# Quarter-array attention, nine-token loads and one set of buffers in an attention and expert-routing kernel

## The chip, the cores and the metric

The kernel runs on 1 core of one Trainium2 chip. The metric is device time in microseconds (us), lower is better. A core has TensorE (PE, matrix products), VectorE (DVE), ScalarE (ACT), GpSimd (POOL), a queue engine (SP), and 16 DMA engines that move data between its memory (SBUF) and DRAM. PE writes its results into PSUM, eight banks of 2 KB a partition; SBUF and PSUM have 128 partitions.

## The reference

```python
# q, k, v: (8 batches, 8 heads, 576 tokens, 64), float32; g_norm: (64,)
kv  = np.einsum('bhsd,bhse->bhde', k, v)
out = np.einsum('bhsd,bhde->bhse', q, kv)
rms = np.sqrt(np.mean(out * out, axis=-1, keepdims=True) + 1e-06)
x   = (out / rms * g_norm)            # transposed and reshaped to (4608 tokens, 512)

logits = x @ w_gate                   # 8 experts
expert_idx = np.argmax(logits, axis=1)
gate_w = softmax(logits)[expert_idx]  # one number a token
for e in range(8):                    # w1: (8, 512, 1024), w2: (8, 1024, 512), float32
    mask = expert_idx == e
    h = np.maximum(x[mask] @ w1[e], 0.0)
    out[mask] = gate_w[mask, None] * (h @ w2[e])
```

Linear attention without a softmax, a norm per head, and then each token goes to one of eight experts. With the given inputs the experts get 564, 494, 600, 572, 539, 654, 585 and 600 tokens.

## The kernel before, in words

The order of the work on every engine is written by hand (`manual_schedule`): each engine does its instructions in the order of the program text, and semaphores hold an instruction until its inputs are there.

**Attention** works in 36 steps `s` of 128 tokens, nine for each pair `P` of batches. `load_qkv` (L157) brings 512 tokens of a batch, four tokens a partition, as rows of 1 KB; `load_rem` (L165) brings the other 64 tokens of two batches as rows of 256 B. All are issued by SP. `heads` (L192) lets POOL copy q into an order by heads. `kv_mm` (L200) multiplies k and v on PE into `kvp`; `kv_copy` (L221), `kv_t` (L227) and `kv_gate` (L235) make from it the blocks `kvs`: for two heads a block diagonal of 128 x 128 and, beside it, 16 columns that give the gate's logits.

A step does: `x_mm` (L267, PE: q transposed times `kvs`, in four products of 128x144), `x_qt` (L251, PE: transposes q for step s + 2), `x_norm` (L284: ACT squares, DVE sums, then in `rest` ACT's Ln and Exp give the inverse root, and DVE writes logits `lr` and tokens `xg` in f16), `x_qs` (L263, ACT: copies the transposed q to SBUF). The lists `mid`, `late` and `last` put the k-v work of later batches, the loads, the casts and the routing into given steps.

`Route` (L318) finds, for nine steps at once (4, 3 and 2 at the end), the best expert of each token (`first`, DVE), its rank among the tokens of that expert (`ranks`, PE), and sends the tokens to rows of `xs_scratch` in DRAM by one indirect DMA of POOL a step (`send`, L386). Unused rows are blanked at the start (L443). After the last step `left_over_table` (L494) finds the tokens over 640 of an expert.

**Experts.** A `Job` (L553) is one expert with room for 5 x 128 = 640 tokens. `fetch` (L562, SP) reads its rows with a transposing DMA; `one` (L581) does four matmuls of 128x320 and ACT's relu; `two` (L600) does eight matmuls of 128x512 for 128 tokens, DVE scales the result, and POOL writes it to its tokens' rows by an indirect DMA (L611). Tokens over the room are done by one more job of 128, ahead of the last expert, and by a loop at the end for further ones. `Weights` (L119): `stage` loads w1 in f32 by SP into one buffer `wst`, `scale` casts it with `g_norm` to f16 (POOL for the first two experts, then DVE), `second` loads w2 by POOL's queue with a cast to f16 on the way. The experts have buffers of their own, which take the place of the attention's when that is closed.

Of the kernel before, what the change touches and what calls it, by code (L numbers as in the profile page):

```python
# [28 lines left out]
def kernel(  # L29
# [20 lines left out]
    CAP = CT * 128  # L50
    NOV = (N - CAP) // 128
# [19 lines left out]
    o = 144 + CT  # L71
    for P in range(4):
        for bb in range(2):
            for j in range(4):
                c32[:, o + 9 * P + 4 * bb + j] = (2 * P + bb) * S + 4 * ar + j
        c32[:64, o + 9 * P + 8] = 2 * P * S + 512 + ar[:64]
        c32[64:, o + 9 * P + 8] = (2 * P + 1) * S + 512 + ar[:64]
# [13 lines left out]
    P_w = ctx.enter_context(tc.tile_pool(name="pw", bufs=1))  # L91

    cf = P_const.tile([128, c32.shape[1]], F32, tag="cf")
    ch = P_const.tile([128, 384], F16, tag="ch")
# [10 lines left out]
    wg = P_const.tile([128, 4, 8], F32, tag="wg")  # L105
    g2 = P_const.tile([128, 1], F32, tag="g2")
    gw = P_const.tile([128, 4, 2, 8], F32, tag="gw")
    epsb = P_const.tile([128, 1], F32, tag="epsb")
    csum = P_const.tile([128, 8], F32, tag="csum")
    valid = P_const.tile([128, E, CT], F32, tag="valid")  # L110
    bigm = P_const.tile([128, E, CT], F32, tag="bigm")
    nvf = P_const.tile([128, 32], F32, tag="nvf")
    tabb = P_const.tile([128, 32], F32, tag="tabb")
    xo_bufs = [P_const.tile([128, RW], F16, tag=f"xo{n}", name=f"xo{n}") for n in range(2)]
    tabi = P_const.tile([128, 2, 32], I32, tag="tabi")
    blank = P_const.tile([96, RW], I32, tag="blank")


    class Weights:  # L119
        def __init__(self, e):  # L120
            self.e = e if isinstance(e, bass.DynSlice) else slice(e, e + 1)

        def stage(self):
            self.st = P_w.tile([128, 4, F], F32, tag="wst", bufs=1, name="wst")
            nc.sync.dma_start(
                self.st, moe_w1[self.e, :, :].rearrange("o (t p) f -> p (o t) f", p=128)
            )

        def scale(self, eng, kk):
            if kk == 0:  # L130
                self.w1 = P_w.tile([128, 4, F], F16, tag="w1e", bufs=3, name="w1e")
            eng.tensor_scalar(  # L132
                self.w1[:, kk, :], self.st[:, kk, :], g2, 1.0, op0=ALU.mult, op1=ALU.mult
            )

        def second(self):
            self.w2 = P_w.tile([128, 8, D], F16, tag="w2e", bufs=3, name="w2e")
            nc.gpsimd.dma_start(
                self.w2, moe_w2[self.e, :, :].rearrange("o (t p) d -> p (o t) d", p=128)
            )  # L140
# [4 lines left out]
    W = [Weights(e) if e != "left" else None for e in order]  # L145

    with (
        tc.manual_schedule(engines=by_hand),
        tc.tile_pool(name="pattn", bufs=1) as PA,
        tc.tile_pool(name="psattn", bufs=1, space=bass.MemoryType.PSUM) as PSA,  # L150
    ):
        kvs_bufs = []
        for n in range(4):
            t = PA.tile([128, 4, 144], F32, tag=f"kvs{n}", name=f"kvs{n}")
            kvs_bufs.append(t)

        def load_qkv(src, b):  # L157
            t = PA.tile([128, 8, 256], F32, tag="ld", bufs=6, name="ld")
            nc.sync.dma_start(
                t, src[b, :, 0:512, :].rearrange("h (p j) d -> p h (j d)", j=4)  # L160
            )
            return t

        def load_rem(src, b0, tag):
            t = PA.tile([128, 8, 64], F32, tag=tag, bufs=2, name=tag)  # L165
            for bb in range(2):
                nc.sync.dma_start(  # L167
                    t[64 * bb:64 * bb + 64, :, :],
                    src[b0 + bb, :, 512:576, :].transpose([1, 0, 2]),
                )  # L170
            return t

        ld, rem, qp, kvst = {}, {}, {}, {}

        def load_batch(b):
            ld["k", b] = load_qkv(k, b)
            ld["v", b] = load_qkv(v, b)
            if b % 2 == 0:
                rem["k", b // 2] = load_rem(k, b, "kr")
                rem["v", b // 2] = load_rem(v, b, "vr")  # L180
            if b == 0:
                nc.sync.dma_start(cf, c_f32.ap())
                nc.sync.dma_start(wg, moe_w_gate.rearrange("(t p) j -> p t j", p=128))
                nc.sync.dma_start(g2[0:64, :], g_norm.unsqueeze(1))
                nc.sync.dma_start(g2[64:128, :], g_norm.unsqueeze(1))
            ld["q", b] = load_qkv(q, b)
            if b % 2 == 0:
                rem["q", b // 2] = load_rem(q, b, "qr")
            if b == 0:
                nc.sync.dma_start(ch, c_f16.ap())  # L190

        def heads(b, j):  # L192

            if j == 0:
                qp[b] = PA.tile([128, 4, 8, 64], F32, tag="qp", bufs=2, name="qp")
            tv = ld["q", b].rearrange("p h (j d) -> p h j d", j=4)
            nc.gpsimd.tensor_copy(qp[b][:, j, :, :], tv[:, :, j, :])  # L197


        def kv_mm(b, i):  # L200
            if i == 0:
                kvst[b] = PSA.tile([128, 4, 64], F32, tag="kvp", bufs=1, name="kvp")
            kvp = kvst[b]
            kb, vb = ld["k", b], ld["v", b]
            kr, vr = rem["k", b // 2], rem["v", b // 2]
            r0 = 64 * (b % 2)
            for j in range(5):
                for hh in range(2):
                    h = 2 * i + hh
                    if j < 4:  # L210
                        lhs = kb[:, h, 64 * j:64 * j + 64]
                        rhs = vb[:, h, 64 * j:64 * j + 64]
                    else:
                        lhs = kr[r0:r0 + 64, h, :]
                        rhs = vr[r0:r0 + 64, h, :]
                    nc.tensor.matmul(  # L216
                        kvp[64 * hh:64 * hh + 64, i, :], lhs, rhs,
                        start=(j == 0), stop=(j == 4),
                    )

        def kv_copy(b):  # L221
            kvp, kvs = kvst[b], kvs_bufs[b % 4]
            for hh in range(2):
                ps = slice(64 * hh, 64 * hh + 64)
                nc.vector.tensor_copy(kvs[ps, :, 64 * hh:64 * hh + 64], kvp[ps, :, :])

        def kv_t(b):  # L227
            kvs = kvs_bufs[b % 4]
            kvtp = PSA.tile([128, 4, 128], F32, tag="misc", bufs=1, name="kvtp")
            for i in range(4):  # L230
                nc.tensor.transpose(kvtp[:, i, :], kvs[:, i, 0:128], ident)
# [220 lines left out]
        for j in range(4):  # L452
            heads(0, j)
# [281 lines left out]
```

## Time and profile before

| | us |
|---|---|
| median of 3 runs (lowest, highest) | 339.13 (336.25, 339.96) |
| the profiled execution, and its span | 340.94, 339.1 |
| first attention product starts, last ends | 23.7, 164.7 |
| first expert matmul starts, last ends | 182.3, 332.8 |
| busy: PE, DVE, ACT, POOL | 263.1, 145.3, 121.9, 118.2 |
| DMA packets, bytes | 84683, 78.30 MB |

The mean granted clock of PE is 0.907 of full speed. A profile line "L278 PE MATMUL" is an instruction of line 278 on PE; "PEld" are the weight loads of PE; an arrow in brackets, as in "[3.82 <-DMA xo", gives the idle time before an instruction and what ended it. In the list of waits the numbers are the sum, how many, and the longest. Matrix products in f32 appear as two records each, transposes and f16 products as one.

### The profile page before, as it was taken

What the parts mean: (1) busy time and instruction counts of PE and PEld (TensorE: products, weight loads), DVE (VectorE), ACT (ScalarE), POOL (GpSimd) and SP (SyncE); (2) the same over time, 40 slices, a digit from 0 to 9 for tenths busy, and PEclk for the clock granted to TensorE, in tenths of its full rate; (3) what the DMA queues carried; (4) which work ended last, traced back from release to release, by engine and by line L of the source; (5) the groups of instructions that cost most, each with busy time, mean ns of one, the idle gap of its engine ahead of it and who ended that gap; (6) DMA issues with size and microseconds to landing.
All of it is one profiled execution on the core that took longest, in us unless ns stands there. A gap on an engine that the chain in (4) does not pass through costs nothing.

```text
span 339.1 us, 5512 instructions
## 1 busy us (share of the span) xinstructions
PE 263.1 (78%) x2119; PEld 187.4 (55%) x2119; DVE 145.3 (43%) x349; ACT 121.9 (36%) x295; POOL 118.2 (35%) x139
## 2 busy tenths in 40 slices
PE   0679499739986798753304999999999999779992
PEld 0578487628875677652202656464747474545650
DVE  0014516814674348578871253343340707054021
ACT  1024526234544354433201607070807070521620
POOL 4022020474117940758420052424250516225123
PEclk9999879987999599969555999999999999979998
DMA  7999999998699989547719978999999995999012
GB/s 237 222 324 305 269 274 350 244 359 286 190 279 342 367 272 226 130 100 151 278 48 181 292 204 154 279 172 265 287 221 327 175 346 158 270 256 223 24 53 95
DMA packets 84683, 78.30 MB, mean 231 GB/s; under 512 B 41771, under 2 KB 75819, under 8 KB 84656
## 3 DMA queue, kind: packets, MB, share of 16 engines
q1 hardware_dynamic: 70240, 54.29, 57.2%
q0 software_dynamic: 14416, 23.65, 30.0%
q8 instruction: 17, 0.28, 0.4%
q14 instruction: 10, 0.08, 0.1%
HBM read 66.46 MB, written 17.09 MB: 246 GB/s over the span
## 4 chain that ended last, share of the span: by engine, by line
PE 29%; DMA 24%; issue 20%; DVE 12%; POOL 6%; SPq 3%; ACT 3%; POOLq 1%; another core or an unknown queue 1%; DVEq 0%
DMA out_dram<-ys,idx 10%; PE op L278 9%; PE yp L603 5%; PE hp L589 5%; DMA xo<-xs_scratch,gi 4%; PE kvp L216 4%; POOL out_dram L611 4%; DMA ld<-in_v_dram 3%; DMA xs_scratch<-blank 3%; PE qtp L260 3%; SPq L167 2%; DMA ld<-in_q_dram 2%; DVE xg L311 2%; DVE dl L332 2%; PE kgp L238 1%
## 5 line engine op out<-in xcount | busy, mean ns | idle before, releaser
L596 ACT ACTIVATE ht<-hp 128x320 f16<-128x320 f32 (+1 forms) x136 | 57.9, 428 | 98.3 <-PE hp L589 62.6
L589 PE MATMUL hp<-xt,w1e 128*128 128x320 f16 (+1 forms) x544 | 76.9, 304 | 11.7 <-DMA xt<-xs_scratch 11.7
L611 POOL DMA_INDIRECT out_dram<-ys,idx x41 | 42.2, 1029 | 112.3 <-DVE ys L608 99.4
L589 PEld LDWEIGHTS <-w1e 128*128 128x128 f16 x544 | 53.3, 100 | 34.8 <-issue 11.8
L603 PE MATMUL yp<-w2e,ht 128*128 128x512 f16 x328 | 72.3, 379 | 0.0
L608 DVE TENSOR_SCALAR ys<-yp,mt 128x512 f32<-128x512 f32 x40 | 29.8, 750 | 91.6 <-PE yp L603 48.5
L278 PE MATMUL op<-kvs,qts 128*128 128x144 f32 (+1 forms) x320 | 51.3, 329 | 8.1 <-issue 5.2
L603 PEld LDWEIGHTS <-ht 128*128 128x128 f16 x328 | 32.1, 98 | 37.3
L386 POOL DMA_INDIRECT xs_scratch<-xg,sli x36 | 35.2, 979 | 50.0 <-DVE sli L384 39.4
L278 PEld LDWEIGHTS op<-kvs,qts 128*128 128x128 f32 (+1 forms) x320 | 43.2, 205 | 11.1 <-issue 6.0
L216 PE MATMUL kvp<-ld 128*64 128x64 f32 x512 | 25.3, 250 | 15.5 <-DMA ld<-in_v_dram 15.5
L197 POOL COPY qp<-ld 128x512 f32<-128x512 f32 x32 | 18.3, 614 | 53.3 <-DMA ld<-in_q_dram 53.2
L294 ACT ACTIVATE sq<-op 128x512 f32<-128x512 f32 x36 | 21.5, 597 | 41.3 <-PE op L278 30.2
L299 DVE TENSOR_REDUCE ms<-sq 128x8 f32<-128x512 f32 x36 | 24.5, 682 | 25.2 <-ACT sq L294 24.1
L265 ACT COPY qts<-qtp 128x512 f32<-128x512 f32 x36 | 21.0, 583 | 35.0 <-PE qtp L260 23.5
L216 PEld LDWEIGHTS kvp<-ld 128*64 128x64 f32 x512 | 20.6, 158 | 20.0 <-issue 19.0
L260 PE MATMUL qtp<-cf,qp 128*128 128x128 f32 x128 | 23.5, 315 | 8.8 <-issue 7.2
L311 DVE TENSOR_TENSOR xg<-op,rinv 128x512 f16<-128x512 f32 x36 | 24.5, 681 | 0.2
L260 PEld LDWEIGHTS qtp<-cf,qp 128*128 128x128 f32 x128 | 18.7, 169 | 9.5 <-issue 7.7
L132 DVE TENSOR_SCALAR w1e<-wst,g 128x1024 f16<-128x1024 f32 x28 | 21.0, 808 | 0.1
L307 DVE TENSOR_TENSOR lr<-op,rinv 128x64 f32<-128x64 f32 x36 | 8.1, 224 | 26.0 <-ACT rinv L305 19.4
L303 ACT ACTIVATE lnt<-ms,epsb 128x8 f32<-128x8 f32 x36 | 10.9, 302 | 11.0 <-DVE ms L299 8.9
(89 smaller groups left out, 143.5 us busy)
## 6 DMA issues: line engine op xcount, KB each, us to landing
wst<-in_moe_w_dram SPq DMA_DIRECT2D x9, 2048.0 KB
w2e<-in_moe_w_dram POOLq DMA_DIRECT2D x9, 1024.0 KB
ld<-in_k_dram SPq DMA_DIRECT2D x8, 1024.0 KB
ld<-in_v_dram SPq DMA_DIRECT2D x8, 1024.0 KB
ld<-in_q_dram SPq DMA_DIRECT2D x8, 1024.0 KB
xs_scratch<-blank SPq DMA_DIRECT2D x8, 193.5 KB
kr<-in_k_dram SPq DMA_DIRECT2D x8, 128.0 KB
vr<-in_v_dram SPq DMA_DIRECT2D x8, 128.0 KB
```

Source lines behind the costliest of these rows:

```text
L216: nc.tensor.matmul(kvp[64 * hh:64 * hh + 64, i, :], lhs, rhs, start=(j == 0), stop=(j == 4),)
L260: nc.tensor.transpose(qtp[:, i, :], src[:, 2 * i:2 * i + 2, :], ident)
L278: nc.tensor.matmul(op[c, i // 2, c0:c0 + 144], qts[s][:, i, c], kvs[:, i, :], start=True, stop=True,)
L294: nc.scalar.activation(sq.rearrange("p (c i h) n -> p c i (h n)", c=2, i=2), oc[:, :, :, 0:128], ACTF.Square,)
L299: nc.vector.reduce_sum(ms, sq, axis=AXX)
L311: nc.vector.tensor_tensor(xg[:, r, 0:512].rearrange("p (c i h n) -> p c i h n", c=2, i=2, h=2), ox, _bc(r4, 4, 64), op=ALU.mult,)
L386: nc.gpsimd.indirect_dma_start(out=xs_views[9 * self.P + g0 + t], out_offset=IndirectOffsetOnAxis(ap=sli[:, t:t + 1], axis=0), in_=xgs[sel ...
L589: nc.tensor.matmul(hp, self.w.w1[:, kk, f * 128:(f + 1) * 128], self.xt[:, kk, ws * wd:(ws + 1) * wd], start=(kk == 0), stop=(kk == 3),)
L596: nc.scalar.activation(self.ht[:, f, ws * wd:(ws + 1) * wd], hp, ACTF.Relu)
L603: nc.tensor.matmul(yp, self.ht[:, f, t * 128:(t + 1) * 128], self.w.w2[:, f, :], start=(f == 0), stop=(f == 7),)
L608: nc.vector.tensor_scalar(ys, yp, self.mt[:, t, 1:2].bitcast(F32), None, op0=ALU.mult)
L611: nc.gpsimd.indirect_dma_start(out=self.views[t], out_offset=IndirectOffsetOnAxis(ap=self.idx[:, t:t + 1], axis=0), in_=ys, in_offset=None ...
```

## The change

- **Loads**: a batch of q, k or v comes as one load of nine tokens a partition, heads of even number on partitions 0 to 63 and odd ones on 64 to 127, in rows of 2304 B; the remainder loads go. The first loads come in halves. They land in ten slots of one tile `land`.
- **Attention in quarters**: all products of the attention are of 64 x 64 in quarters of the array, with heads apart instead of as block diagonals; the transposes of q are products with the identity that read `land`, so the copies by POOL go. Per step 16 calls for `x_mm` (72 columns) and 16 for `x_qt`; 72 k-v calls a batch.
- **PSUM and SBUF** have one set for all stages: `ps_q` (one buffer for transposed q, two before), `ps_kv`, `ps_o[0]`, `ps_o[1]`, two f16 buffers each for w1 and w2, and `xh`, which holds `xg` in attention and `ht` later.
- **Weights** come both in f32, issued by ACT, into five slots of `land` that are free; five loads start in steps 29 to 34. DVE casts w1, ACT casts w2; ACT casts both for the first expert.
- **Routing** is cut finer and spread over steps; POOL's queue blanks the scratch rows.
- **Room**: 608 tokens an expert instead of 640, products of 304 columns.

```diff
-    CAP = CT * 128
+    CAP = 608
+    WIDTHS = [128, 128, 128, 128, 96]
...
+    land = fixed("land", [128, 10, LW], F32)
+    stg = [land[:, 2 * n:2 * n + 2, :].rearrange("p a c -> p (a c)")[:, 0:4 * F]
+           for n in (2, 3, 0, 1, 4)]
+    ps_q = PS.tile([128, 2, 512], F32, tag="ps_q", name="ps_q")
+    ps_kv = PS.tile([128, 2, 512], F32, tag="ps_kv", name="ps_kv")
+    ps_o = [PS.tile([128, 2, 512], F32, tag=f"ps_o{n}", name=f"ps_o{n}") for n in range(2)]
+    hp_banks = [ps_q[:, 0, :], ps_q[:, 1, :], ps_kv[:, 0, :], ps_kv[:, 1, :]]
+    yp_banks = [ps_o[0][:, 0, :], ps_o[0][:, 1, :], ps_o[1][:, 0, :], ps_o[1][:, 1, :]]
...
+        def cast1(self, kk):
+            nc.vector.tensor_scalar(
+                self.w1[:, kk, :], self.s1[:, kk, :], g2, 1.0, op0=ALU.mult, op1=ALU.mult
+            )
+        def cast1_act(self, kk):
+            nc.scalar.mul(self.w1[:, kk, :], self.s1[:, kk, :], g2)
+        def cast2(self, kk):
+            nc.scalar.copy(self.w2[:, 2 * kk:2 * kk + 2, :], self.s2[:, 2 * kk:2 * kk + 2, :])
...
+    def load_next(count=1):
+                (W[n].load1 if m == 1 else W[n].load2)(stg[n_loads % 5], nc.scalar)
...
+    def load(name, b, parts=1):
+        n = {"k": (2 * b) % 6, "v": (2 * b + 1) % 6, "q": 6 + b % 4}[name]
+        view = src[b].rearrange("(i hh) (p j) d -> (hh p) i (j d)", hh=2, j=9)
...
+    def kv_mm(b, ip):
+        for j in range(9):
+            js = slice(Dh * j, Dh * j + Dh)
+            for hh in range(2):
+                for ipar in range(2):
+                    i = 2 * ip + ipar
+                    nc.tensor.matmul(
+                        ps_kv[HALF[ipar], hh, Dh * ip:Dh * ip + Dh],
+                        kb[HALF[hh], i, js], vb[HALF[hh], i, js],
+                        start=(j == 0), stop=(j == 8),
+                    )
...
+    def x_qt(s):
+        for tok in range(2):
+            for ip in range(2):
+                c0 = 64 * (2 * tok + ip)
+                for hh in range(2):
+                    for ipar in range(2):
+                        nc.tensor.matmul(
+                            ps_q[HALF[ipar], hh, c0:c0 + 64],
+                            qb[HALF[hh], 2 * ip + ipar, Dh * j:Dh * j + Dh],
+                            ident[HALF[hh], HALF[hh]], start=True, stop=True,
+                        )
...
+    def x_mm(s):
+        for ip in range(2):
+            for hh in range(2):
+                for ipar in range(2):
+                    for tok in range(2):
+                        nc.tensor.matmul(
+                            op[HALF[tok], ipar, c0:c0 + 72],
+                            qts[s][HALF[ipar], hh, q0:q0 + 64],
+                            kvs[HALF[ipar], ip, hh, :], start=True, stop=True,
+                        )
...
             f = first_slot[b]
+            at(late, f - 4, kv_mm, b, 0)
+            at(late, f - 3, kv_mm, b, 1)
             at(last, f - 3, kv_copy, b)
             at(late, f - 2, kv_t, b)
             at(mid, f - 1, kv_gate, b)
...
+                at(late, s + 1, rt.peak)
+                at(late, s + 2, rt.choose)
+                at(last, s + 2, rt.ranks)
+                at(last, s + 3, rt.weigh)
+                at(last, s + 3, rt.send)
...
+        at(last, 1, load_all, ("k", 4), ("v", 4))
+        at(last, 6, load_all, ("q", 4), ("k", 5), ("v", 5), ("q", 5))
+        at(last, 10, load_all, ("k", 6), ("v", 6))
+        at(last, 15, load_all, ("k", 7), ("v", 7), ("q", 6), ("q", 7))
+        at(last, 29, load_next, 2)
+        at(last, 31, load_next, 2)
+        at(last, 34, load_next, 1)
...
+        for kk in range(4):
+            W[0].cast1_act(kk)
+        count()
+        left_over_table()
...
+        jobs[0].fetch()
+        jobs[1].fetch()
+        for kk in range(4):
+            W[0].cast2(kk)
+        load_next(2)
...
+            for ws in range(job.halves):
+                    job.one(ws, f)
+                    if ws == 0 and f % 2 == 1 and nxt is not None:
+                        W[n + 1].cast1(f // 2)
...
+            if nxt is not None:
+                load_next()
+            for t in range(job.nt):
+                job.two(t)
+                if nxt is not None and t < 4:
+                    W[n + 1].cast2(t)
...
+                load_next()
```

## The prediction, made before the change was run

> **What bounds the kernel now.** I read the page first, then the engine and transfer shares by stage, then the timeline of three stages, the waits, and last single records of the trace (starts of matmuls and weight loads, DMA packets by size).
>
> ```profile
> span 339.1 us, 5512 instructions
> PE 263.1 (78%) x2119; PEld 187.4 (55%) x2119; DVE 145.3 (43%) x349; ACT 121.9 (36%) x295; POOL 118.2 (35%) x139
> ...
> PE   0679499739986798753304999999999999779992
> ...
> PEclk9999879987999599969555999999999999979998
> DMA  7999999998699989547719978999999995999012
> ```
>
> The slices (8.5 us each) show two stages: attention to slice 20, where PE has holes, and the experts from slice 22, where PE is full. The timeline dates them: the first attention product (L278) starts at 23.7 us, the last ends at 164.7, the first expert matmul starts at 182.3, the last ends at 332.8. So the span is 23.7 start + 141.0 for 36 attention steps + 17.6 passage + 150.5 experts + 6.3 end = 339.1. The profiled execution took 340.94, the median of the three runs is 339.13; I sum against the span and take the sum as the time (1.8 us more is inside the range).
>
> ```profile
> 26.74 0.69 PE L216 MATMUL kvp<-ld 128*64 128x64 f32 x16
> ...
> 27.35 0.33 PE L216 MATMUL kvp<-vr,kr 64*64 64x64 f32 x4
> ...
> 33.14 0.60 ACT L294 ACTIVATE sq<-op 128x512 f32<-128x512 f32 x1 [1.47 <-PE op L278]
> ...
> 35.05 0.58 ACT L294 ACTIVATE sq<-op 128x512 f32<-128x512 f32 x1
> ...
> 37.47 0.60 ACT L294 ACTIVATE sq<-op 128x512 f32<-128x512 f32 x1
> ```
>
> One square (L294) opens each step, so their starts give the step. Steps without k-v products take 1.91 to 2.41 us (here 33.14, 35.05, 37.47); steps with them 3.4 to 4.1; the average is 141.0/36 = 3.9. What a clean step consists of is a ring through ACT and DVE: square 0.60, sum 0.68, Ln 0.30, Exp 0.21, two products 0.23 and 0.68 on DVE.
>
> ```profile
> ACT qts L265 <- remote: 11.0, 3, 5.1
> ...
> DVE kvs L241 <- remote: 7.2, 2, 5.3
> ...
> ACT sq L294 <- remote: 6.5, 2, 3.2
> ```
>
> ```profile
> 157.07 4.48 DVE L332 TENSOR_TENSOR dl<-lg,mx 128x24 f32<-128x24 f32 x1
> 157.11 4.40 POOL L132 TENSOR_SCALAR w1e<-wst,g 128x1024 f16<-128x1024 f32 x4
> ```
>
> Four further holes are seen. Three lie beside the bursts of nine scatters (L386, 65 to 76, 101 to 112, 136 to 147 us): signals from PE reach ACT and DVE up to 6 us late. The fourth is a DVE operation that took 4.48 us instead of 0.18 while POOL scaled weights.
>
> ```profile
> 219.28 8.86 PE L589 MATMUL hp<-xt,w1e 128*128 128x320 f16 x64
> ...
> 227.97 8.80 PE L603 MATMUL yp<-w2e,ht 128*128 128x512 f16 x40
> ...
> 236.60 8.86 PE L589 MATMUL hp<-xt,w1e 128*128 128x320 f16 x64
> ...
> 298.55 0.40 PE L630 MATMUL xp<-ch,xo 128*128 128x128 f16 x4 [3.82 <-DMA xo<-xs_scratch,gi]
> ```
>
> The experts are bound by PE: one takes 17.32 us (219.28 to 236.60), with one hole of 3.8 us.
>
> **Part 1, start.** Now the first k-v product waits until 10.45 us for all of k0 and v0, then remainder rows of 256 B come in between. After, it waits for half of each, 1.18 MB: at the 353 GB/s of 4 to 8 us that is 3.3 us after a first packet near 3, so about 8; the second half by 11. From the end of these products to the first x_mm it took 6.3 us (17.4 to 23.7). With q0 landed near 14.5 I take **18.5** (5.2 less). Ends: 16 to 22.
>
> **Part 2, attention steps.** Calls of 64x64x64 or 64x64x72 on quarters: 72 for k-v, 72 for q transposes and 72 for x_mm per batch, and 16 small ones: 232. No row shows four quarters. The nearest: in the trace the records of L216 start in pairs 6 to 7 ns apart, pairs every 58 ns warm; a call is two records, so a call costs 58 ns, and the 64*64 rows say the same (55). If pairs are two column halves at work together, each half takes 116 ns a call, and four quarters give 29. So 29 to 58 ns. I take 29: the 6 ns starts show that two records do run together, and consecutive calls always change quarter.
> The page TensorE: Matmul & The Clock Gate (Part 1) of the Trainium skill states that start-to-start never drops below about 25 ns; that would make 50 ns a call and 309 us. The 6 to 7 ns of the trace speak against it.
> At 29 ns PE needs 0.93 us for a step and 1.05 more for one with half a batch of k-v products: 1.98, under the ring's 2.2. So each step goes by the ring, whose shapes (512 elements) do not change: 36 x 2.2 = 79.2. The copies of q (L197, 18.3 us on POOL) leave; the transposes read the landing buffer. DVE's routing work, 4.5 us for nine groups by its rows (L326 1.19, ten of about 0.23, and the small ones), is spread over three steps but stays on DVE, which is in the ring: three times 3, and two small ones of 2, is 13. PE no longer stands behind the routing chain (it waited 10.4 us for `cs` at L352), but ranks still waits for kv_copy; that is within the 13. The scatter bursts stay: three times 4 is 12 (0 to 15). The 4.48 leaves, since POOL computes nothing more. Sum 79.2 + 13 + 12 = **104.2**. Ends: 84 with no stalls and half the routing; at 58 ns a k-v step takes 3.95, that is 1.75 more in 16 steps, 132.
> Transfers as cover: q, k, v in 24 x 512 rows of 2304 B. 1 KB rows alone ran at 350 GB/s (24 to 28 us), 4 KB rows at 400 (164 to 168). At about 370, 28.3 MB take 76 us, with blank, constants and scatters some 92, and the buffers let about four batches be ahead. Step 27 needs the last k and v near 85 us; it comes near 100. Hidden, but not by much: it forbids less than 84 for the steps.
>
> **Part 3, passage.** Five weight loads (10.5 MB, 26 us at 400 GB/s) start at step 29, near 101, and end near 127, before the experts. ACT now issues them and makes eight casts of the first expert; a cast of 1024 elements is 0.97 us by the slope from 320 (0.438) to 512 (0.583), together 7.8, plus issues: done 13 us after the last product, just inside the passage. `fetch` no longer waits for the table on DVE (SP's 2.5 us for `tabi` L533). 17.6 - 2.5 = **15.1**. Ends: 14 to 20, where ACT's issues wait for queue space (on SP, transposes queued behind a weight load took 10 to 16 us to issue instead of 2.6).
>
> **Part 4, experts.** 304 columns instead of 320 in 64 matmuls: 8.86 x 16/320 = 0.44 less, times 8, 3.6 less. The second products keep 512 columns and their 40. One tile is left over by the given inputs, before (expert 5 has 654 over 640) and after (over 608), so the loop at the end does not run. ACT gets four casts of w2 an expert, 3.9 us, in the 8.8 us when it has no relu; DVE keeps four casts of w1. The hole of 4 goes: w2 leaves the queue of the scatters. 150.5 - 3.6 - 4.2 = 142.7. But w2 now lands in f32 and POOL's queue gets only scatters: 13 loads x 2.1 MB at 400 is 68, eight transposing fetches of 2432 packets at 837 a us 23, seven experts' outputs 21, the rest 4: 116 us for the 121 until the last expert starts. That is nearly full, so I add 3 (0 to 15): **145.7**. End **6.3** as now.
>
> **Sum.** 18.5 + 104.2 + 15.1 + 145.7 + 6.3 = 289.8; I say **289**.
>
> **Rivals.** (a) *Two quarters at a time*, 58 ns a call: 28 us more, **317**. For it: the only 64x64 rows; against: the 6 ns starts. (b) *Weights come late*: ACT's issue blocks for queue space or 2 KB rows run like 1 KB ones; per expert two loads 12, fetch 3, output 3, and waiting, 19 instead of 16.9, seven times: 15 more, **304**. For it: the transposes' 10 to 16 us of issue; against: a lead of two experts. (c) *Slower*: **each change of row half drains the array**. The trace prices a change of shape from 128*64 to 64*64 at 205 instead of 58 ns between weight loads, 147 more. The order of calls changes the row half after every two calls: (116 + 147)/2 = 131 ns a call, 232 x 8 x 131 ns = 243 us for attention: 18.5 + 243 + 15.1 + 142.7 + 6.3 = **426**. It decides from 84 ns a call (156 us of steps, what the other parts leave up to 339). Against it: in the change the shape itself never changes, which is what drained here.
> The page TensorEngine Tiling (Array Packing) of the skill (Restrictions and Gotchas) adds that different row tiles cannot use one PSUM bank at once; kv_t and kv_gate do that in 16 of 232 calls. No row shows it.
> (d) *Attention is bound by transfers*, everything else as hoped: steps 84, no stalls: **267**.
>
> **Chances.** Forecast 0.62, (a) 0.18, (b) 0.07, (c) 0.08, (d) 0.05. About 1 % is what a measurement of this kernel can tell from no change. Only (c) is slower; a point each for same and slower from (a) and (b) together. Faster 0.89, same 0.02, slower 0.09. The range from 265 to 320 takes in (d), (b) and (a) and leaves out (c) and the tails.
>
> **What would show it.** Right: squares 2.0 to 2.4 us apart in nearly all steps, k-v steps too; four weight loads of the new L-lines starting within 20 ns; the first expert matmul at 130 to 145 us; then 16.9 us an expert with holes of under 5 us. Wrong: k-v steps near 4 us (a); ACT busy or waiting in casts while PE idles between experts (b); gaps over 80 ns between calls on quarters (c). POOL copies, "remote" waits outside the scatter bursts, or a second table load would each be a surprise.

## The result, and the profile after

The changed kernel takes 413.0 us (411.9 to 414.9) beside 339.5 of the kernel before on the same chip: ratio 1.219, interval 1.211 to 1.227. It is 22 per cent slower, where 289 us were forecast. The profiled execution took 411.9, its span is 410.0. The executions of a kernel fall into a faster and a slower group, and every ratio below compares the faster ones.

The first lines of its page: the span, PE's busy time, PE's busy tenths in 40 slices of 10.25 us, PE's granted clock, the DMA engines.

```profile
span 410.0 us, 10466 instructions
...
PE 250.2 (61%) x4631; PEld 175.0 (43%) x4631; DVE 136.4 (33%) x343; ACT 156.9 (38%) x335; POOL 89.0 (22%) x91
...
PE   2374756674667653000777777877878778776770
...
PEclk9967577989598975555799999999999999999995
DMA  7999958639412099999439597695969954020020
```

PE has twice the records of before (4631 for 2119) and less busy time (250 for 263). There are some 5000 more instructions, and in no slice is PE full. Before, the expert slices read 9; now most read 7 and 8. By the forecast's stages:

| stage | before | forecast | measured | missed by |
|---|---|---|---|---|
| start to the first x_mm (L290) | 23.7 | 18.5 | 23.4 | 4.9 |
| 36 attention steps | 141.0 | 104.2 | 137.4 | 33.2 |
| passage to the first expert product | 17.6 | 15.1 | 33.0 | 17.9 |
| experts | 150.5 | 145.7 | 204.5 | 58.8 |
| end | 6.3 | 6.3 | 11.7 | 5.4 |

The misses add up to 120.2, from 289.8 to the span of 410.0.

**Attention.** The timeline of the changed kernel shows products and squares of two steps, with some rows left out (start, duration, engine, line; in brackets the idle time and what ended it):

```profile
30.58 0.60 ACT L305 ACTIVATE sq<-ps_o 128x512 f32<-128x512 f32 x1 [3.94 <-PE ps_o L290]
...
31.10 1.18 PE L214 MATMUL ps_kv<-land 64*64 64x64 f32 x34
34.86 0.74 PE L214 MATMUL ps_kv<-land 64*64 64x64 f32 x34 [2.58 <-issue]
...
36.46 0.60 ACT L305 ACTIVATE sq<-ps_o 128x512 f32<-128x512 f32 x1 [3.98 <-PE ps_o L290]
...
37.84 0.56 PE L290 MATMUL ps_o<-kvs,qts 64*64 64x72 f32 x6
41.22 0.53 PE L290 MATMUL ps_o<-kvs,qts 64*64 64x72 f32 x18 [2.82 <-issue]
```

The quarters do what was forecast: four records in a row start within 20 ns, and a call costs 30 ns at full clock (54 at half clock), where the forecast had 29. But PE stops in the middle of a series, here for 2.6 and 2.8 us, and waits for nothing that the profile shows ("issue"). In the list of matmuls the first stops stand at numbers 349, 477, 605, 733 and 860: one after every 128 records (127 once), that is 64 calls of two products and two weight loads each, or 256 instructions. At each stop the trace has one packet of 16384 B on the queue for instructions (32.48 to 33.57 us, 38.62 to 39.71), and PE goes on 1.2 to 1.6 us after the end of the packet. In the steps there are 28 such packets, and PE stops at 20 of them. After each stop of 1.8 us or more the granted clock goes to half within 1.5 us, or is there already (the slices of 5 to 7).

The waits of PE, the longest lines that matter (sum, how many, longest):

```profile
PE ps_q L506 <- DMA xt<-xs_scratch: 25.6, 1, 25.6
PE ps_q L506 <- ACT xh L513: 19.1, 34, 2.3
PE ps_kv L506 <- ACT xh L513: 17.2, 34, 0.6
PE ps_o L290 <- issue: 14.6, 7, 3.4
PE ps_o L526 <- DVE ys L531: 13.5, 16, 0.8
PE ps_kv L214 <- issue: 12.8, 9, 2.6
...
PE ps_q L269 <- issue: 7.1, 4, 3.7
```

The stops come to 34.4 us, the passage to one wait of 25.6 us, and the experts to 68 waits for the relu and 16 for the scaling. The stops are not all that the steps lost. PE is busy for 86.8 us of the 137.4, while the 1740 or so calls of the steps at 30 ns would be 52; the granted clock, 0.79 on average in the steps, is a part of that. And PE waits another 16 us, nearly all of it for other engines.

**Passage.** The queues of ACT and SP, and the first expert product:

```profile
160.40 0.37 ACTq L152 DMA_DIRECT2D land<-in_moe_w_dram  x1
...
169.58 0.37 ACTq L158 DMA_DIRECT2D land<-in_moe_w_dram  x1
...
175.66 12.80 SPq L485 DMA_TRANSPOSE xt<-xs_scratch  x1
...
179.93 0.38 ACTq L152 DMA_DIRECT2D land<-in_moe_w_dram  x1
...
193.82 1.17 PE L506 MATMUL ps_q<-xt,w1b 128*128 128x304 f16 x4 [25.57 <-DMA xt<-xs_scratch]
```

The last scatter is issued at 169.49, and the fetch, which waits until it has landed, starts only at 175.66. This transposing fetch then takes 12.80 us to issue, beside two or three weight loads of 2 MB. In the kernel before, with nothing else on the queues, it took 2.53.

**Experts.** A group is four products into one bank. Here are three groups, of which the last two share a tile of two banks:

```profile
195.50 1.17 PE L506 MATMUL ps_q<-xt,w1b 128*128 128x304 f16 x4 [0.51 <-ACT xh L513]
...
196.47 1.22 PE L506 MATMUL ps_kv<-xt,w1b 128*128 128x304 f16 x4
...
198.20 1.17 PE L506 MATMUL ps_kv<-xt,w1b 128*128 128x304 f16 x4 [0.51 <-ACT xh L513]
```

The second group in a tile waits until ACT has read the first; the first group of the other tile does not. An expert takes 24.28 us, six times over, where it took 17.32 before and 16.9 in the forecast.

### The profile page after: what moved, and what is told of

The parts are those of the page before. It is cut to its first block, busy times and chain, and to the rows that moved or that the text cites. A ratio compares the mean times of both kernels' runs of the same rounds, so it can differ in the third digit from the quotient of the medians.

```text
span 410.0 us, 10466 instructions
## 1 busy us (share of the span) xinstructions
PE 250.2 (61%) x4631; PEld 175.0 (43%) x4631; DVE 136.4 (33%) x343; ACT 156.9 (38%) x335; POOL 89.0 (22%) x91
## 3 DMA queue, kind: packets, MB, share of 16 engines
q0 software_dynamic: 5472, 15.85, 10.8%
## 4 chain that ended last, share of the span: by engine, by line
issue 47%; DMA 19%; PE 15%; POOL 11%; DVE 4%; ACT 2%; POOLq 1%; SPq 0%; DVEq 0%
DMA out_dram<-ys,idx 11%; POOL out_dram L534 8%; DMA land<-in_v_dram 6%; PE ps_o L290 5%; PE ps_kv L214 5%; PE ps_q L269 4%; POOL xs_scratch L400 3%; DMA xs_scratch<-xh,sli 2%; DVE xh L321 1%; PE ps_kv L232 1%; ACT sq L305 1%; DVE ms L309 1%; PE ps_kv L243 0%; POOLq L534 0%; DVE lr L317 0%
## 5 line engine op out<-in xcount | busy, mean ns | idle before, releaser
L506 PEld LDWEIGHTS <-w1b 128*128 128x128 f16 x544 | 52.5, 99 | 93.5 <-issue 75.0
L526 PE MATMUL ps_o<-w2b,xh 128*128 128x512 f16 (+1 forms) x328 | 74.8, 379 | 13.5 <-DVE ys L531 13.5
L506 PE MATMUL ps_q<-xt,w1b 128*128 128x304 f16 (+1 forms) x272 | 46.2, 293 | 44.6 <-DMA xt<-xs_scratch 25.6
L400 POOL DMA_INDIRECT xs_scratch<-xh,sli x36 | 34.8, 966 | 129.1 <-DVE kvs L248 116.5
L506 PE MATMUL ps_kv<-xt,w1b 128*128 128x304 f16 (+1 forms) x272 | 46.0, 292 | 17.2 <-ACT xh L513 17.2
L526 PEld LDWEIGHTS <-xh 128*128 128x128 f16 (+1 forms) x328 | 33.6, 103 | 51.8 <-issue 17.9
L290 PE MATMUL ps_o<-kvs,qts 64*64 64x72 f32 x1152 | 38.5, 269 | 19.3 <-issue 14.6
L269 PE MATMUL ps_q<-cf,land 64*64 64x64 f32 x1152 | 35.7, 267 | 14.4 <-issue 7.1
L290 PEld LDWEIGHTS ps_o<-kvs,qts 64*64 64x64 f32 x1152 | 31.9, 170 | 21.6 <-issue 15.7
L513 ACT ACTIVATE xh<-ps_kv 128x304 f16<-128x304 f32 (+1 forms) x68 | 28.2, 414 | 29.7 <-PE ps_kv L506 26.8
L269 PEld LDWEIGHTS ps_q<-cf,land 64*64 64x64 f32 x1152 | 30.6, 175 | 15.8 <-issue 7.9
L171 ACT CAST w2b<-land 128x1024 f16<-128x1024 f32 x36 | 34.9, 1041 | 0.6 <-issue 0.2
L309 DVE TENSOR_REDUCE ms<-sq 128x8 f32<-128x512 f32 x36 | 24.5, 681 | 30.1 <-ACT sq L305 28.4
L278 ACT COPY qts<-ps_q 128x512 f32<-128x512 f32 x36 | 21.0, 584 | 21.5 <-PE ps_q L269 21.5
L321 DVE TENSOR_TENSOR xh<-ps_o,rinv 128x512 f16<-128x512 f32 x36 | 24.5, 680 | 0.0
(85 smaller groups left out, 115.9 us busy)
## 6 DMA issues: line engine op xcount, KB each, us to landing
land<-in_v_dram SPq DMA_DIRECT2D x7, 1152.0 KB, 16.1
```

What stands on the lines that cost most here:

```text
L171: nc.scalar.copy(self.w2[:, 2 * kk:2 * kk + 2, :], self.s2[:, 2 * kk:2 * kk + 2, :])
L269: nc.tensor.matmul(ps_q[HALF[ipar], hh, c0:c0 + 64], qb[HALF[hh], 2 * ip + ipar, Dh * j:Dh * j + Dh], ident[HALF[hh], HALF[hh]], start=Tru ...
L290: nc.tensor.matmul(op[HALF[tok], ipar, c0:c0 + 72], qts[s][HALF[ipar], hh, q0:q0 + 64], kvs[HALF[ipar], ip, hh, :], start=True, stop=True,)
L309: nc.vector.reduce_sum(ms, sq, axis=AXX)
L321: nc.vector.tensor_tensor(xg[:, r, 0:512].rearrange("p (c i n) -> p c i n", c=2, i=4), oc[:, :, :, 0:64], _bc(r4, 3, 64), op=ALU.mult,)
L400: nc.gpsimd.indirect_dma_start(out=xs_views[9 * self.P + g0 + t], out_offset=IndirectOffsetOnAxis(ap=sli[:, t:t + 1], axis=0), in_=xgs[sel ...
```

## The experiments

The theory is that there are three separate causes. In the experts it is the tiles of two banks, within which a product waits for the reader of the other bank. In attention, PE runs out of instructions. In the passage, weight loads stand in front of the fetch. Rivals stand in the expectations.

The runs fell on four chips: A (e5 to e8), B (e1 to e4), C (e9 to e16), D (e17, e18). On A the steps of the unedited kernel are like those above; on the others three steps are longer, of which e17 and e18 tell, so steps are compared on one chip only. (The passage is shorter where the steps take longer, 21 to 27 us where this part is unedited, instead of 33 to 36; probably more of the weights has landed by then, which no run shows by itself.)

Stages are those of the profiled execution. PE's stops by "issue" in the steps come in two kinds: those after which PE goes on 1.0 to 1.75 us after the end of a 16 KB packet, and the others, which all but two lie beside POOL's scatters.

| run | steps | PE's stops: after a packet + others | passage | an expert | median | ratio to before |
|---|---|---|---|---|---|---|
| unedited, as above | 137.4 | 34.4 + 0 | 33.0 | 24.3 | 413.0 | 1.219 (1.211 to 1.227) |
| e1 banks | 164.2 | 31.5 + 20.5 | 24.7 | 18.0 | 379.7 | 1.119 (1.100 to 1.138) |
| e2 late weights | 167.5 | 30.2 + 20.7 | 15.1 | 24.3 | 429.8 | 1.269 (1.248 to 1.291) |
| e3 halves | 152.2 | 4.6 + 15.5 | 26.8 | 24.3 | 423.6 | 1.250 (1.234 to 1.267) |
| e4 all three | 155.1 | 8.8 + 16.1 | 15.2 | 18.0, then holes | 403.1 | 1.189 (1.167 to 1.211) |
| e5 unedited, A | 136.9 | 31.6 + 0 | 35.9 | 24.3 | 414.7 | two executions |
| e6 plain writes | 144.6 | 36.5 + 0 | 26.0 | 24.3 | 407.7 | 1.202 (1.194 to 1.210) |
| e7 no loads | 115.9 | 21.0 + 0 | 35.3 | 24.3 | 395.2 | one execution |
| e8 early weights | 130.8 | 6.9 + 0 | 16.1 | 18.0, then holes | 391.6 | 380 to 403 us |
| e9 single banks | 164.7 | 30.1 + 18.8 | 24.7 | 16.9, then holes | 409.8 | 1.223 (1.203 to 1.243) |
| e11 | 171.6 | 18.7 + 11.4 | 15.2 | 16.9, then holes | 385.1 | 1.138 (1.111 to 1.166) |
| e13 unedited, C | 162.9 | 28.5 + 20.1 | 24.5 | 24.3 | 431.4 | 1.288 (1.258 to 1.318) |
| e15 | 158.4 | 8.4 + 14.0 | 15.1 | 18.0 | 361.7 | 1.080 (1.060 to 1.100) |
| e17 plain writes, D | 147.7 | 34.5 + 0 | 21.0 | 24.3 | 407.6 | one execution |
| e18 unedited, D | 163.6 | 27.4 + 17.8 | 25.2 | 24.3 | 431.2 | one execution |

The executions of e8, e10, e12 and e16 lie 4 to 9 per cent apart, so their spread is given and no ratio. Of e11 and e15 one execution in four is 9 and 12 per cent above the fastest.

**e1, order of the banks.**

```diff
-    hp_banks = [ps_q[:, 0, :], ps_q[:, 1, :], ps_kv[:, 0, :], ps_kv[:, 1, :]]
+    hp_banks = [ps_q[:, 0, :], ps_kv[:, 0, :], ps_q[:, 1, :], ps_kv[:, 1, :]]
```

and so for `yp_banks`.

> Theory A: the experts take 24.3 us each instead of the forecast 16.9 because two neighbouring groups of products use the two banks of one PSUM tile, so a product into the second bank waits for the relu (or the scaling) that reads the first. With the order of the banks alternating between tiles the waits of L506 on xh (36 us in all) and of L526 on ys (13.5 us) vanish, an expert takes 17 to 18.5 us, and the time is about 365 us (355 to 372). Rival B: ACT is too slow in the experts (its four casts of w2 stand between the relus), whatever the bank: period stays above 23, 408 to 415 us.

An expert takes 17.99 us, five times over (a sixth 18.21). Of the 36 us of waits for the relu 2.2 are left. Here is the timeline of e1, consecutive groups:

```profile
233.91 0.68 PE L506 MATMUL ps_q<-xt,w1b 128*128 128x304 f16 x4
...
234.43 0.68 PE L506 MATMUL ps_kv<-xt,w1b 128*128 128x304 f16 x4
...
235.10 0.68 PE L506 MATMUL ps_q<-xt,w1b 128*128 128x304 f16 x4
```

Rival B is out: ACT with all its casts keeps up. The 1.1 us over 16.9 are the same wait in small: the starts are 0.52 and 0.67 us apart, since a tile still has to be read before its other bank is written (with single banks, in e9, an expert takes 16.90). The time, 379.7, lies above the expected 355 to 372 because this chip's steps are 27 us longer than in the profile above; the passage gives back 8.

**e2, late weights.** The load of step 34 and the two after the first expert's casts are left out there, and three loads go out after the second relu instead.

> Theory A: the 33 us between the last x_mm and the first expert product are long because weight loads on ACT's queue fill the DMA engines while the scatters land and the transposing fetch is issued (12.8 us of issue). With no load of the third expert before the second relu of the first one, the issue of the first fetch takes about 2.5 to 4 us, the scatters land 2 to 3 us earlier, the passage is 18 to 22 us and the time 398 to 403 us. Rival B: the fetch is slow by itself (its source has just been written): passage above 29, 408 us or more.

```profile
201.23 2.51 SPq L485 DMA_TRANSPOSE xt<-xs_scratch  x1
...
205.79 1.17 PE L506 MATMUL ps_q<-xt,w1b 128*128 128x304 f16 x4 [8.50 <-DMA xt<-xs_scratch]
```

The fetch issues in 2.51 us and the passage is 15.1, as the prediction had it, so weight loads beside the fetch are shown as the cause. The time did not follow, for two reasons: the longer steps of this chip, and 6 us lost in the first expert, where three weight loads issued by ACT (the third blocked it for 5.2 us) delay the relus.

**e3, fewer calls.** The q transposes over all 128 rows, the x products with 128 columns, with another order of columns in `ps_q` (the calls in short form, not as the code has them):

```diff
-   16 x matmul(ps_q[HALF[ipar], hh, c0:c0+64], qb[HALF[hh], i, 64 cols], ident[HALF[hh], HALF[hh]])
+    8 x matmul(ps_q[HALF[ipar], 0, c0:c0+128], qb[:, i, 64 cols], ident)
-   16 x matmul(op[HALF[tok], ipar, c], qts[HALF[ipar], hh, 64 cols], kvs)
+    8 x matmul(op[:, ipar, c], qts[HALF[ipar], hh, 128 cols], kvs)
```

> The same products of attention in fewer calls: the q transposes use 128 rows and the x products 128 columns, 164 instead of 232 calls a batch; the k-v products stay as they are. Theory A: PE runs out of instructions after every 64 calls (256 instructions) and stands 2.2 to 3.7 us until the next 16 KB have come; 29 such stops become about 20, PE's idle time by issue falls from 34 to 20 to 25 us, the 36 steps go from 136 to 115 to 127 us, the time is 390 to 403 us. Rival B: the steps wait for transfers of q, k and v, and the stops of PE only fill that time: steps 132 us or more, 407 us or more. Rival C: pairs of half-array calls run slower than four quarters: steps over 140 us.

```profile
PE ps_kv L214 <- issue: 7.1, 12, 2.0
...
PE ps_o L290 <- issue: 6.8, 9, 1.1
PE ps_q L268 <- issue: 6.3, 4, 3.2
```

On the same chip the steps go from 164.2 and 167.5 (e1, e2) to 152.2, and the stops after a packet from 31 to 4.6 us; what is left of the stops lies beside the scatters. So theory A is right about the stops. About the time it is not: of some 31 us of stops in all that are gone, the steps get 12 to 15 shorter, for PE needs longer for its work. A record of these calls costs 55 and 56 ns instead of 15. The sums in the expectation assumed the steps of chip A, where e8 has the same edit: there the stops fall from 31.6 to 6.9 us, PE's busy time rises from 87.1 to 117.6 and the steps fall by 6.1 only, to 130.8, against the 115 to 127 expected (e8 also loads weights from step 20 on). The first twelve steps, before the first scatter, took 42.9 us against 53.6 and 53.8 in e1 and e2.

**e4, the three together.**

> The three edits together: bank order, late weight loads, fewer calls. Theory A (three separate causes): the gains add up, 48 + 12 + 15 us, to 333 to 345 us. Rival B: with the experts at 17 us each the weight loads or the fetches come too late and 5 to 15 us come back: 346 to 360 us, with PE waiting for DMA or casts between experts.

The passage is 15.2. The first expert loses 7 us as in e2, and the others take 18 to 19 us but for two of 26.1 and 40.5. This is rival B, and worse than it said. PE waits for DVE's scaling, which waits for a free buffer of the output scatters (10.8 us at the longest), while SP's transposing fetches take 19 to 30 us to issue.

**e5, the unedited kernel again, and e6, no scatters**, both ran on chip A.

> The changed kernel once more, unedited. In the runs with another bank order and with late weights the 36 steps took 164 and 167 us instead of 137, though nothing before step 34 was edited: while POOL issues nine scatters, PE gets through only eight to ten instructions per 1.4 us. Theory A: this depends on the chip or on where the program lies: here the steps take 160 to 170 us too and the time is 435 to 445 us. Theory B: it belongs to those kernels: 137 us and 411 to 415 us as before.

> The 36 scatters of tokens are left out; in their place SP writes the same rows to fixed places with plain transfers, and every expert is given 576 tokens (so the output is not that of the reference). POOL issues nothing during attention. Theory A: POOL's nine scatters in a row hold up PE; without them no step takes over 6.5 us, the stretches with 0.4 to 1.1 us between x products are gone, and the steps take 105 to 125 us, what is left being the stops for instructions (25 to 35 us). Theory B: the slow stretches come from the transfers themselves or from PE: they stay, and the steps take 137 us or more.

e5 has steps of 136.9 us and takes 411 to 418: theory B as far as this chip goes (e13 corrects it). In e6 the steps take 144.6, so the expected 105 to 125 are missed. As this chip shows no slow stretches with the scatters either, that they are absent here tells nothing. Step 29 alone takes 13 us: ACT stands at the issue of a weight load for 11 us, until plain writes have landed.

**e7, no loads of batches 3 to 7.**

> The loads of q, k and v of batches 3 to 7 are left out (the landing buffers keep the first batches, so the output is not that of the reference); the DMA engines are idle from about 35 us until the weights. Theory A: PE's stops at every 64 calls are waits for instructions: they stay where they are, though shorter where the 16 KB no longer stand behind loads (1.2 to 2.2 us instead of 2.2 to 3.7), and the first twelve steps take 42 to 50 us instead of 54. Theory B: the stops are waits for q, k and v in disguise: they vanish, and the first twelve steps take 26 to 32 us.

```profile
PE ps_kv L219 <- issue: 10.8, 9, 3.0
...
PE ps_o L295 <- issue: 5.0, 4, 1.7
PE ps_q L274 <- issue: 3.1, 5, 1.1
...
PE ps_kv L237 <- issue: 2.0, 1, 2.0
```

The stops stay at the same matmuls, and once the loads have ended those at 605, 733, 860 and 1116 take 0.8 to 1.2 us instead of 2.2 to 3.4. The packet itself takes about 1.1 us in both. But in e7 it starts 1.2 to 1.8 us before PE stops, and beside the loads between 0.1 us before and 0.9 us after. The first twelve steps take 42.0 us. This is theory A, and it splits the miss of 33.2. Without these transfers the steps take 115.9, so 21.5 us belong to the transfers: 13.4 by shorter stops, and 10.4 by PE's own time (76.5 us busy at a granted clock of 0.89 instead of 86.8 at 0.79), less 2 of other waits that are added. The 18 us of stops after the loads have ended need no loads.

**e8, early weights.** This is e1 and e3 together, with weight loads in steps 20, 25, 28 and 33 and two more after the second relu.

> Bank order and fewer calls as before; the first five weight loads go out as soon as their buffers are free (steps 20, 25, 28 and 33 instead of 29, 31 and 34), and the next two wait for the second relu of the first expert. Theory A: the transfers of the experts are then ahead enough: passage 15 to 18 us, experts 18 us each without holes, the time 358 to 375 us (with attention as slow as in the last runs, 150 to 160 us). Rival B: the late two loads push the transposing fetches back again, with holes of 5 us or more between experts: above 380 us.

It takes 391.6 us (379.8 to 402.8), so rival B, with experts of 30, 31 and 48 us among those of 18.

**e9, tiles of one bank in the experts.**

```diff
+        PX = ctx.enter_context(tc.tile_pool(name="psumx", bufs=1, space=bass.MemoryType.PSUM))
+        for n in range(4):
+            hp_banks.append(PX.tile([128, 512], F32, tag=f"hp{n}", name=f"hp{n}"))
+            yp_banks.append(PX.tile([128, 512], F32, tag=f"yp{n}", name=f"yp{n}"))
```

> The experts get eight PSUM tiles of one bank each (a pool of their own, opened when attention's is closed); nothing else is changed. Theory A: the tile of two banks is the whole cause of 24.3 us an expert: now PE waits for no relu and no scaling, an expert takes the forecast 16.9 us (up to 17.3), and the time falls by 7 times 7.3 and by some 7 in the last expert, from 413 to 350 to 358 us. Rival B: at this pace the transfers are the limit, and an expert takes 18 us as with the other bank order: 360 to 366 us.

Experts 2 and 3 take 16.90 us, so the forecast's 16.9 was right for PE, and the tile of two banks is the whole of the 7.4 us that an expert takes longer in the changed kernel. Then four take 24.4 to 27.4, which neither theory had. PE waits there for DVE's scaling, as in e4. The DMA queues of e9 (queue, packets, MB, share of 16 engines in the window), at 248 to 264 us and then in a hole, 278 to 296:

```profile
q10 hardware_dynamic: 1268, 3.58, 70.0%
q0 software_dynamic: 384, 1.01, 17.2%
q1 hardware_dynamic: 1325, 0.34, 14.0%
```

```profile
DMA packets 2220, 1.03 MB, mean 57 GB/s; under 512 B 2060, under 2 KB 2060, under 8 KB 2220
...
q1 hardware_dynamic: 2045, 0.51, 111.1%
q0 software_dynamic: 48, 0.15, 9.7%
q10 hardware_dynamic: 127, 0.36, 5.0%
```

A packet of the transposing fetch (q1) takes 0.14 x 256 / 1325, 27 ns, and in the hole 1.111 x 288 / 2045, 156 ns; the engines are taken up by them, and all queues together move 57 GB/s.

**e10 to e12, combinations with single banks.** All have early weight loads, none extra before the first expert, and blank rows written after step 0; e11 also has x products of 128 columns, e12 the halves of e3.

> Single banks; the first five weight loads early (steps 20, 25, 28, 33) and none of the next two before the first expert (two an expert, as later on); blank rows written after step 0 instead of at the start. Attention stays in quarters. Theory A: q0 comes 3 to 4 us earlier, the steps take about 135 us, the passage 15 to 17 us, an expert 17 to 18 us without holes: 325 to 342 us. Rival B: weight loads and transposing fetches collide as in the run with early weights, with holes of 10 us or more between experts: above 350 us.

> As the last, and the x products with 128 columns a call (eight calls instead of sixteen in 32 of 36 steps): 200 instead of 232 calls a batch. Theory A (stops for instructions): 25 instead of 29 stops, but each x product group takes 0.4 us more of PE; the steps are 3 to 8 us shorter than with quarters. Rival B (PE's own time decides): 5 to 14 us longer.

> As the one before the last, and attention with 164 calls a batch (q transposes over 128 rows, x products with 128 columns). Theory A: the stops nearly vanish (under 10 us in all), PE needs some 0.8 us more in each step, and the steps take 126 to 132 us; in all 318 to 336 us. Rival B: with the weights now landing during attention the stops come back: 137 us or more of steps, 330 us or more.

e10 takes 410 us (389 to 417), e11 385.1, e12 382.5 (380 to 414). In all three, one to four experts lose 9 to 17 us in holes, and the passage is 15.1 to 15.2. That is rival B for e10. For e11 it is neither: the steps are 1.7 us shorter than in e10. For e12 rival B fits in its numbers (160.6 us of steps) and not in its reason: the stops after a packet stay at 6.4 us, and 13.5 lie beside the scatters. Later blank rows bring the first x_mm to 18.8, 19.2 and 19.9 us, where the prediction had 18.5. So the 1.6 MB of blanks beside q0 were what it left out.

**e13 and e14, unedited and "spread" scatters**, ran on chip C.

> The changed kernel once more, unedited, beside the next run on the same chip. If this chip is like that of the first runs: 411 to 418 us and steps of 137 us; if like the two others: 430 to 445 us, with 7 to 17 us in steps 13, 22 and 31.

> Two scatters at step 3 and two at step 4 after each group of nine, then one a step, in place of nine in a row; nothing else. Theory A (the burst makes PE slow): on a chip where the kernel above shows steps of 7 to 17 us they are gone, and it is 15 to 28 us faster than the kernel above; on a chip without them it is within 5 us of it. Theory B (a single scatter slows PE as much): the same time is lost in more steps, no difference over 5 us.

They take 431.4 and 429.5 us. In e13, the unedited kernel, steps 13, 22 and 31 take 10.4, 10.3 and 12.1 us, as long as in e1. So the chip decides and not the edit of e1 or e2. The edit of e14 misses its aim: nothing holds POOL back, so it issued the moved scatters one behind the other all the same (every 1.27 us). It allows no verdict.

**e15 and e16, combination with the bank order**: the second also has the moved scatters.

> Bank order (not single banks), halves in attention, the first five weight loads early, none of the next two before the first expert, blank rows after step 0. Theory A: at 18 us an expert the fetches keep up, as in the first run with the bank order: start 19, steps 131 (150 on a chip with slow steps), passage 16, then 165 us: 331 us (350 us). Rival B: the holes come from the short passage (loads still under way when the fetches start) and not from the pace: 350 us or more (370 or more), with holes over 8 us.

> The last kernel with the scatters spread as two runs above. Theory A: no step over 7 us on any chip: 325 to 340 us if the experts have no holes; in any case not slower than the last kernel by over 3 us. Rival B: no difference from the last kernel over 5 us on a chip with slow steps.

e15 takes 361.7 us, and the profiled execution has experts of 18.0 to 19.3 and 20.3 us without a hole. That is theory A, 12 us over its figure for such a chip, 8 of them in the steps. But a fourth execution took 401.6, and no trace says where; holes as in rival B would fit. e16 takes 383 to 400 us, and neither of its theories holds: steps 13 and 22 still take 8.7 and 10.9 us, and its profiled execution has holes of 12 and 25 us. Since it has the pace of e15, the pace alone does not keep the holes away. e15 is the best version found: 361.7 beside 431.4 for the changed kernel on this chip, and still 8 per cent slower than the kernel before.

**e17 and e18, with and without scatters on chip D.**

> Again the kernel without scatters (SP writes the rows to fixed places, every expert gets 576 tokens, so the output is not that of the reference). If the kernel below has steps 13, 22 and 31 of 7 us or more on this chip: Theory A (POOL's scatters slow PE): none of them is over 5.5 us here, steps 20 to 28 us less in all than below. Theory B (the chip, whatever POOL does): they stay at 10 to 12 us. If the kernel below has none, nothing is decided.

> The changed kernel, unedited, for the comparison with the run above: 137 us of steps on a chip like the first one's, 162 to 166 us on a chip with slow steps.

Here is one x product group of step 13 with scatters (e18):

```profile
83.06 0.96 POOL L400 DMA_INDIRECT xs_scratch<-xh,sli  x1 [0.30 <-issue]
83.36 0.55 PE L290 MATMUL ps_o<-kvs,qts 64*64 64x72 f32 x5 [0.18 <-issue]
...
84.83 0.52 PE L290 MATMUL ps_o<-kvs,qts 64*64 64x72 f32 x5 [0.92 <-issue]
...
86.25 0.51 PE L290 MATMUL ps_o<-kvs,qts 64*64 64x72 f32 x4 [0.91 <-issue]
...
92.01 0.59 ACT L278 COPY qts<-ps_q 128x512 f32<-128x512 f32 x1 [8.76 <-remote]
```

and the same group without them (e17):

```profile
83.85 0.60 ACT L305 ACTIVATE sq<-ps_o 128x512 f32<-128x512 f32 x1 [1.76 <-PE ps_o L290]
...
84.43 1.18 PE L290 MATMUL ps_o<-kvs,qts 64*64 64x72 f32 x31
84.70 0.59 ACT L278 COPY qts<-ps_q 128x512 f32<-128x512 f32 x1 [0.26 <-PE ps_q L269]
```

Steps 13, 22 and 31 take 10.3, 11.0 and 12.0 us with scatters and 1.8, 2.0 and 4.7 without: theory A on this chip, 24.7 us less in these three. (Of these, 10 come back in step 29, as in e6, so all the steps together are 16 us shorter.) PE gets four or five records done per 1.4 us while POOL issues scatters, and ACT's copy of `ps_q`, whose products on PE are done by 83.2 us in e18, starts only at 92.0.

## Why the prediction was wrong, point by point

- **What it had right.** Four quarters work at once, 30 ns a call. Rivals (a) and (c) did not occur, so the one slower rival was the wrong one. Nor did (b): PE waits for no weights. The transfers are ahead: in the steps PE waits 1.3 us for q, k and v. ACT's issues and casts are as priced (a cast 1.04 us for 0.97). Three more terms come out where nothing else stands in their way: 16.9 us an expert (e9), 18.8 to 19.9 us of start (e10 to e12), a passage of 15.1 (e2, e10, e15).
- **Experts, 58.8 us: a missing term.** The step "142.7" counted instructions and never asked what the one set of buffers does to the waits on PSUM. Two banks of one tile count as one for waiting: 24.28 us instead of 16.9 (e1, e9), 7.4 in each of seven experts, 52 of the 58.8. The added 3 us for full transfers was too small as well: at 16.9 an expert, experts of 24 to 34 us follow in e9 and e10.
- **Attention, 33.2 us: the step "each step goes by the ring".** Only 10 of 35 squares follow 1.8 to 2.4 us after the one before, where it had nearly all. It priced a call by its start-to-start time at full clock and not the 928 instructions a batch that PE has to be given. A block of 256 lasts 1.9 us at 30 ns a call, less than the 2.3 to 3.2 us from the start of its packet until PE goes on. The Trainium skill (Runtime: NRT & Kernel Launch, Instruction fetch mechanics) says that instructions come in blocks of 16 KiB, 256 in each, and that the cost of crossing a block is mostly hidden. The blocks are as the trace shows them. Hidden they are not here: 34.4 us of stops in 20 places. Before, where the fastest 128 records take 9.5 us, one of ten packets in the steps has a stop, of 0.8 us. That the stops are about as large as the miss does not make them the whole of it, since PE's longer busy time and its other waits stand beside them. How much of the 33.2 would go with the stops alone stays open: in e8 25 us of stops went and 6 us of the steps.
- **Scatters, a term of 12 in the same sum.** It fits neither kind of chip. On A steps 13, 22 and 31 take 1.8, 2.0 and 6.9 us with scatters (e5) and 1.8, 2.0 and 4.7 without (e6), so 2 us; on D it is 25. In the profile before, PE itself stands still for 12.4 us by "issue" beside the three bursts, which the prediction read as late signals.
- **Passage, 17.9 us: the cover ran out.** The step "end near 127, before the experts" took the five loads alone and an attention of 104 us. Two more loads follow the casts, and all use the DMA engines that the scatters and the fetch need. The prediction looked for harm in ACT's issues, which took 0.4 us each; it was in SP's, 12.80 us. It had the row for that, SP's transposes of 10 to 16 us behind a weight load, and used it for ACT only.
- **Start, 4.9 us: the term "q0 landed near 14.5".** The k-v products start as forecast, at 7.4 and 11.5 us, but the first transpose waits for q0 until 20.7 (15.8 in e10). The 1.6 MB of blank rows on POOL's queue compete with q0; they were counted in the total and not here.
- **End, 5.4 us.** No run tries this. POOL's last scatter waits 2.69 us for an earlier one to land.
- **Two small slips of the sum.** Half a batch of k-v products falls in 14 steps and not 16, so rival (a) would cost 25 us and not 28; and the longest of the late signals in its rows is 5.3 us and not 6.

**What stays open**: why single transposing packets go from 27 to 156 ns in some experts and executions, why a scatter slows PE on some chips and not on others, why the packet of instructions starts later beside loads, and what the end costs.

## What to carry to other kernels

Count instructions as well as cycles: when calls get small, ask how long 256 of them last, and look for stops at equal numbers of instructions that wait for nothing. Fewer, larger calls remove such stops, but look at what the calls then cost: here 25 us of stops less made the steps 6 us shorter on one chip, and some 31 us less made them 12 to 15 shorter on another. When buffers are merged, write down for each wait which tile it is on, not which bank; alternating the tiles brought an expert from 24.28 to 17.99 us. A transfer that nothing waits for still takes the engines of one that everything waits for: hold it back until the urgent one is issued, but not so long that the next stage has no lead.

## What the runs showed of the hardware that was not expected

- Matmul records on quarters most often start 6 to 7 ns apart, and 15 ns apart on average over 60 of them. The 25 ns floor between starts that the Trainium skill states without an exception (TensorE: Matmul & The Clock Gate, Part 1) does not hold between quarters here.
- One 16 KB block of instructions costs a stop of 2.2 to 3.4 us beside loads at 390 GB/s and 0.8 to 1.2 us at the same four places without them; the packet itself takes about 1.1 us in both.
- A call on half the array does the work of two calls on quarters and costs more than both: a record with 128 rows and 64 columns, or 64 rows and 128 columns, costs 55 and 56 ns in e3, one on a quarter 15.
